# Output of a sparse-attention and mixture-of-experts kernel gathered per token chunk as whole rows, and written after the last column block

## The chip, the cores and the metric

One core of one Trainium2 chip. The metric is the device time of one execution in microseconds, as the median of several runs. The tensor engine (TensorE, PE in the rows), the vector engine (VectorE, DVE), the scalar engine (ScalarE, ACT), GpSimd (POOL) and the sync engine (SyncE, SP), whose queue issues all of this kernel's transfers, run beside each other and wait for one another by semaphores.

## The reference

Attention over 4 batches, 8 heads, 576 positions and 64 dimensions, half of the heads with a local mask, half with a strided one. Its output `x` (2304 tokens, 512 columns) goes through a dense layer pair and then through a soft mixture of experts, whose end is what the change is about:

```python
h = x @ w_in
g = h * (1.0 / (1.0 + np.exp(-1.702 * h)))
x = g @ w_out                                   # 2304 x 512
logits = x @ phi                                # 2304 x 32
d = softmax over the tokens of logits
slot_input = d.T @ x                            # 32 x 512
for e in range(8):                              # 4 slots per expert
    slot_out[e] = np.maximum(slot_input[e] @ w1[e], 0.0) @ w2[e]
c = softmax over the slots of logits
out = c @ slot_out                              # 2304 x 512, float32
```

## The kernel before, in words

Attention and the first dense layer run over five chunks of tokens (`CHUNKS`: four of 512 and one of 256). The slots' sums are gathered on the way, so that the last 55 us hold only the experts and the combination. There the work is set by the order in which the program is written; nothing reorders it but a scheduler that places TensorE's instructions by their readiness.

- The expert weights come in 32 tiles `ex` of 1 MiB (128 partitions, 8 KB each), loaded by SyncE's queue (line 487) as buffers come free. Tiles 4 to 19 of the list are the first expert layer (`expand1`, line 639), tiles 20 to 35 the second (`expand2`, line 669).
- The second layer is cut into three column blocks of the 512 output columns (`COLS`: 256, 128 and 128 wide) that use eight, four and four tiles. In the code `half` counts these blocks, 0 to 2. When a block's tiles are done, `slot_out` (lines 674 and 675) turns the sums into the slot outputs `so`, stored in the tile `fin`, first on ScalarE, then on VectorE.
- `combine` then multiplies the tokens' weights `cT0`/`cT1` (transposed by `combine_t`, cast out of PSUM at line 626) by `so`: one matmul per 128 tokens and column block (line 686), into PSUM tiles `fp` of 512 columns, three buffers of them. Each `fp` is copied to SBUF, in turn by ScalarE (line 689) and VectorE (line 691), and written to `out` (line 692).
- A call of `combine` takes two or four groups of 128 tokens (`PARTS` for the first two blocks, `LAST` for the third) and a staging slot from `gx_tile`, which hands out four regions of the tile `gT` in rotation. Five calls per block, so 15 calls use the four regions in turn, and the copy into a region waits until the region's earlier write has landed.
- A write has rows of 1 KB (block 0) or 512 B (blocks 1 and 2) in `out`, with 128 consecutive tokens on the 128 partitions.
- The combination of block 0 stands between the tiles of block 1, that of block 1 between the tiles of block 2, that of block 2 at the end.

Of the kernel before, what the change touches and what calls it, by code (L numbers as in the profile page):

```python
# [9 lines left out]
F32 = mybir.dt.float32  # L10
# [9 lines left out]
NT, DM, FF = B * S, 512, 2048  # L20
# [9 lines left out]
CHUNKS = [(0, 512), (512, 512), (1024, 512), (1536, 512), (2048, 256)]  # L30
NF = FF // 128
TFROM = 5
COLS = [(0, 256), (256, 128), (384, 128)]
PARTS = [(0, 2), (2, 4), (6, 4), (10, 4), (14, 4)]
LAST = [(0, 4), (4, 4), (8, 4), (12, 4), (16, 2)]
# [6 lines left out]
def tile_kernel(ctx: ExitStack, tc: tile.TileContext, lqk, lv, sqk, sv, wraw, phi, wexp, cst, out):  # L42
    nc = tc.nc
    P = 128
# [4 lines left out]
    xp = ctx.enter_context(tc.tile_pool(name="xp", bufs=3))  # L49
# [302 lines left out]
    side, st, todo = [], {}, []  # L352
# [123 lines left out]
    def gx_tile():  # L476
        k = gxn[0] % 4
        gxn[0] += 1
        return gt[0][:, 4 * k:4 * k + 4]
# [95 lines left out]
    c = len(CHUNKS) - 1  # L575
# [26 lines left out]
    cT0 = tl.tile([P, 2048], F32R, name="cT0")  # L602
# [3 lines left out]
    def ttile(name):  # L606
        return ps_t.tile([P, 512], F32, tag="t", name=name)
# [13 lines left out]
    def combine_t(c):  # L621
        c0, N = CHUNKS[c]
        ctp = ttile(f"ctp_{c}")
        for tt in range(N // 128):
            nc.tensor.transpose(ctp[:, 128 * tt:128 * tt + 128], c4s[c][:, 128 * tt:128 * tt + 128], ident)
        nc.scalar.copy(cT0[:, c0:c0 + N] if c < 4 else cT1, ctp[:, :N])

    hzt = e1p.tile([P, 2, 8, P], F32, tag="e", name="hz")
    hc = e1p.tile([P, 4, 512], F32, tag="e", name="hc")
# [28 lines left out]
    ops, obs = [], {}  # L658

    def expand2(half, n):  # L660
        c0, w = COLS[half]
        per = DM // w
        if n == 0:
            ops.append(mtile(f"op_{half}"))
        t = ex[20 + c0 // 32 + n].rearrange("p j f -> p (j f)").rearrange("p (k j f) -> p k j f", k=per, j=4)
        for k in range(per):
            G, fc = (per * n + k) // 8, (per * n + k) % 8
            for j in range(4):
                nc.tensor.matmul(ops[half][32 * j:32 * j + 32, :w], hz[G][:, fc, 32 * j:32 * j + 32], t[:, k, j], start=G + fc == 0, stop=G + fc == 8)  # L669

    def slot_out(half):
        c0, w = COLS[half]
        o = ops[half][:, :w]
        nc.scalar.mul(so[:, 0, c0:c0 + w], o, zc[:, 0:1])
        nc.vector.scalar_tensor_tensor(so[:, 1, c0:c0 + w], o, zc[:, 1:2], so[:, 0, c0:c0 + w].bitcast(F32), op0=ALU.mult, op1=ALU.add)

    def combine(half, k, n):
        c0, w = COLS[half]
        per = DM // w
        ob = gx_tile().rearrange("p a b -> p (a b)")[:, :n * w].rearrange("p (t f) -> p t f", f=w)  # L680
        for a in range(0, n, per):
            z = min(n, a + per)
            fp = ttile(f"fp_{half}_{k}_{a}")[:, :w * (z - a)].rearrange("p (t f) -> p t f", f=w)
            for t in range(a, z):
                tok = P * (k + t)
                nc.tensor.matmul(fp[:, t - a], cT0[:, tok:tok + P] if k + t < 16 else cT1[:, tok - 2048:tok - 2048 + P], so[:, 1, c0:c0 + w], start=True, stop=True)
            obs[0] = not obs.get(0)
            if obs[0]:
                nc.scalar.copy(ob[:, a:z], fp)
            else:  # L690
                nc.vector.tensor_copy(ob[:, a:z], fp)
        nc.sync.dma_start(out[P * k:P * (k + n), c0:c0 + w].rearrange("(t p) f -> p t f", p=P), ob)

    expand1(0, 0)
    hz = [hzt[:, 0], hzt[:, 1]]
# [11 lines left out]
    for c in range(2):  # L707
        combine_split(c)
        combine_t(c)
# [10 lines left out]
    so, cT1 = fin[:, :2], fin[:, 2, :256]  # L720
    hidden_t(1, 0)
    for n in range(8):
        expand2(0, n)
        if n == 2:
            hidden_t(1, 1)
        if n >= 5:
            combine_split(n - 3)
            combine_t(n - 3)
    slot_out(0)
    for half in range(1, len(COLS)):  # L730
        todo = list(PARTS)
        tiles = COLS[half][1] // 32
        for n in range(tiles):
            expand2(half, n)
            if n:
                for _ in range(-(-len(todo) // (tiles - n))):
                    combine(half - 1, *todo.pop(0))
        slot_out(half)
    for k, n in LAST:
        combine(len(COLS) - 1, k, n)  # L740


def _layouts(q, k, v, w_in, w_out, phi, w1, w2):
# [63 lines left out]
```

## Time and profile before

| | us |
|---|---|
| median of three runs | 442.29 |
| lowest, highest | 441.05, 443.08 |
| profiled execution | 440.19 |
| its span, first to last instruction | 438.4 |
| TensorE busy in the span | 413.0 (94%) |
| VectorE, ScalarE, GpSimd busy | 264.4, 194.1, 77.2 |
| moved by DMA | 80.90 MB |

The span is measured inside the profiled execution, and 1.8 us of that execution lie around it. TensorE's busy time is an average over stages with different limits; what the change is worth is read from the last 30 us alone. Times in the rows are microseconds from the span's start, and durations of single instructions are in ns where a view says so.

### The profile page before, as it was taken

How to read it: one execution, taken by the hardware profiler on the slowest of the kernel's cores; microseconds unless marked ns; L12 is line 12 of the kernel's file. 1: busy time of each engine (PE TensorE's matmuls, PEld its weight loads, DVE VectorE, ACT ScalarE, POOL GpSimd, SP SyncE). 2: the span in 40 equal slices, each digit the busy share in tenths (PEclk: the TensorE clock that was granted, in tenths of full speed). 3: DMA queues.
4: the chain of work that ended last, by engine and by line, in shares of the span. 5: the costliest groups of instructions: out<-in, count | busy, mean ns of one | idle time of the engine just before them, and what ended most of it. 6: DMA issues, size and time to landing. Idle time of an engine off the chain costs nothing.

```text
span 438.4 us, 10081 instructions
## 1 busy us (share of the span) xinstructions
PE 413.0 (94%) x4085; PEld 282.0 (64%) x4085; DVE 264.4 (60%) x564; ACT 194.1 (44%) x640; POOL 77.2 (18%) x96
## 2 busy tenths in 40 slices
PE   8978998998899999999999999999999999899965
PEld 4646575656466767677676776776777796244654
DVE  2789989998996554565467546546454664431212
ACT  2874877766664644454543355331122222120312
POOL 0444445555531110100100001000000000100000
PEclk9999999999999999999999999999999999999995
DMA  8957667676753030321411101770003898979998
GB/s 245 362 169 243 224 201 257 232 239 224 236 171 121 1 101 2 91 78 56 154 42 58 38 1 37 270 305 1 1 0 108 298 381 324 346 310 428 426 351 250
DMA packets 25614, 80.90 MB, mean 185 GB/s; under 512 B 2144, under 2 KB 9440, under 8 KB 21472
## 3 DMA queue, kind: packets, MB, share of 16 engines
q1 hardware_dynamic: 25568, 80.26, 52.2%
q8 instruction: 32, 0.52, 0.5%
q14 instruction: 14, 0.11, 0.1%
HBM read 71.34 MB, written 8.91 MB: 183 GB/s over the span
## 4 chain that ended last, share of the span: by engine, by line
PE 69%; DVE 10%; ACT 8%; DMA 4%; POOL 4%; issue 4%; ACTq 0%; POOLq 0%; DVEq 0%
PE h L321 38%; PE u L435 5%; PE s L163 4%; DMA out<-gT 4%; ACT ts L181 4%; PE lg L340 4%; PE hp L639 3%; DVE wc L264 3%; PE op L669 2%; PE av L218 2%; PE ptp L199 2%; POOL ts L184 2%; PE busy L78 2%; DVE wc L265 2%; POOL wc L262 1%
## 5 line engine op out<-in xcount | busy, mean ns | idle before, releaser
L321 PE MATMUL h<-x,wi 128*128 128x512 f32 (+1 forms) x960 | 224.5, 380 | 4.4 <-POOL wi L273 1.7
L321 PEld LDWEIGHTS h<-x,wi 128*128 128x128 f32 x960 | 161.6, 189 | 54.1 <-issue 13.8
L325 DVE SCALAR_TENSOR_TENSOR gT<-gT,h 128x512 f32<-128x512 f32 (+1 forms) x64 | 40.6, 634 | 61.9 <-ACT gT L324 61.2
L324 ACT ACTIVATE gT<-h 128x512 f32<-128x512 f32 (+1 forms) x64 | 35.6, 556 | 68.1 <-PE h L321 66.4
L181 ACT ACTIVATE ts<-ts,nmx 128x64 f32<-128x64 f32 (+1 forms) x120 | 41.6, 349 | 28.6 <-DVE nmx L176 28.2
L184 POOL TENSOR_TENSOR ts<-ts,sm 128x384 f32<-128x384 f32 (+2 forms) x32 | 27.9, 873 | 139.2 <-DVE sm L183 65.4
L348 DVE STREAM_TRANSPOSE gT<-gT 128x512 f32<-128x512 f32 (+1 forms) x64 | 41.0, 649 | 0.9
L262 POOL TENSOR_SCALAR wc<-wc 128x512 f32<-128x512 f32 x32 | 24.5, 765 | 28.4 <-ACT wc L261 26.0
L340 PE MATMUL lg<-gT,wp 128*32 128x512 f32 (+1 forms) x128 | 26.9, 564 | 0.3 <-ACT wp L297 0.3
L264 DVE SCALAR_TENSOR_TENSOR wc<-raw,wc 128x512 uint32<-128x512 uint32 x32 | 26.0, 817 | 0.4
L265 DVE SCALAR_TENSOR_TENSOR wc<-raw,wc 128x512 uint32<-128x512 uint32 x32 | 25.4, 794 | 0.3
L163 PEld LDWEIGHTS s<-qk 64*64 64x64 f32 x552 | 20.9, 133 | 6.4 <-issue 5.0
L163 PE MATMUL s<-qk 64*64 64x96 f32 (+1 forms) x552 | 25.0, 235 | 0.0
L273 POOL TENSOR_TENSOR wi<-wc,wi 128x512 fp32r<-128x512 f32 x16 | 22.2, 1388 | 15.5 <-ACT wi L272 15.3
L243 ACT CAST x<-av 128x320 fp32r<-128x320 f32 (+20 forms) x54 | 19.1, 395 | 13.0 <-DVE x L244 9.6
L261 ACT ACTIVATE wc<-raw 128x512 f32<-128x512 f32 x32 | 21.7, 678 | 5.7 <-DMA raw<-wraw 5.6
L263 DVE TENSOR_SCALAR wc<-wc 128x512 uint32<-128x512 uint32 x32 | 20.1, 628 | 6.6 <-POOL wc L262 6.5
L182 DVE TENSOR_SCALAR sm<-sm 128x5 f32<-128x5 f32 (+2 forms) x32 | 6.8, 213 | 27.5 <-ACT ts L181 27.5
L181 ACT ACTIVATION_READ_ACCUMULATOR ts<-ts,nmx 128x1 f32 x120 | 22.6, 188 | 0.0
L199 PE MATMUL ptp<-cs,ts 128*96 128x128 f32 (+1 forms) x120 | 17.7, 280 | 4.9 <-POOL ts L184 4.5
L435 PE MATMUL u<-gT,dT 32*32 32x512 f32 x576 | 20.2, 597 | 2.1 <-DVE z L410 2.1
L697 POOL MEMSET hz<- 128x512 f32 x4 | 2.1, 560 | 110.7 <-PE spp L592 110.7
(124 smaller groups left out, 472.6 us busy)
## 6 DMA issues: line engine op xcount, KB each, us to landing
ex<-wexp SPq DMA_DIRECT2D x28, 1024.0 KB, 7.9
raw<-wraw SPq DMA_DIRECT2D x32, 512.0 KB, 4.4
qk<-lqk SPq DMA_DIRECT2D x8, 592.0 KB, 5.4
wo_scr<-wc SPq DMA_DIRECT2D x16, 256.0 KB, 2.9
ex<-wo_scr SPq DMA_DIRECT2D x4, 1024.0 KB, 9.2
gT<-wexp SPq DMA_DIRECT2D x4, 1024.0 KB, 5.8
qk<-sqk SPq DMA_DIRECT2D x6, 604.0 KB, 4.1
v<-lv SPq DMA_DIRECT2D x8, 432.0 KB, 4.5
```

Of the source, the lines that this page charges most:

```text
L163: nc.tensor.matmul(sp[hs, u], t[hs, qo:qo + 64], t[hs, ko + qo:ko + qo + nk], start=not early, stop=not early or u == nt - 1)
L181: nc.scalar.activation(ts[:, u], src[:, u], AF.Exp, scale=sc, bias=nmx[:, u:u + 1], accum_out=sm[:, u:u + 1])
L184: nc.gpsimd.tensor_tensor(ts, ts, sm[:, :nt].unsqueeze(2).to_broadcast([P, nt, nk]), op=ALU.mult)
L262: nc.gpsimd.tensor_scalar(t, t, F64_LARGE, F64_SMALL, op0=ALU.min, op1=ALU.max)
L264: nc.vector.scalar_tensor_tensor(u, raw[:, :, 1], 0xC0000000, u, op0=ALU.bitwise_and, op1=ALU.bitwise_or)
L265: nc.vector.scalar_tensor_tensor(u, raw[:, :, 0], 29, u, op0=ALU.logical_shift_right, op1=ALU.bitwise_or)
L321: nc.tensor.matmul(h[:, :N], w[:, we, 128 * kt:128 * kt + 128], x[xe][:, kt, :N], start=n == 0, stop=n == 11)
L324: nc.scalar.activation(g[:, :N], h[:, :N], AF.Tanh, scale=0.851)
L325: nc.vector.scalar_tensor_tensor(g[:, :N], g[:, :N], 1.0, h[:, :N], op0=ALU.add, op1=ALU.mult)
L340: nc.tensor.matmul(lgs[c][32 * j:32 * j + 32, :N], wp[:, f0 + j, :], gs[c, f0 + j][:, :N], start=f0 == 0, stop=f0 == NF - 4)
L348: nc.vector.transpose(t_slots(c)[:, f, :N], gs[c, f][:, :N])
L435: nc.tensor.matmul(us[a][32 * j:32 * j + 32, :].rearrange("p (t f) -> p t f", f=32), dT[q, 32 * b:32 * b + 32], gT[q, :, 32 * b:32 * b + 3 ...
```

## The change

`combine` now takes a chunk of tokens instead of a list of groups. Each of the five chunks has a region of its own for its output, which holds all 512 columns: the four regions of `gT` for the chunks of 512 tokens, and a new tile `ob_last` for the chunk of 256. All three column blocks are copied into it, and the write is issued when the third has been copied. The tokens of a chunk are dealt to the partitions differently: partition p holds the four tokens 4p to 4p+3 of the chunk (two in the last), so that a partition's part of `out` is one stretch of 8 KB (4 KB). For that, `combine_t` stores the columns of `cT0` and `cT1` in another order, while they are cast.

```diff
-        nc.scalar.copy(cT0[:, c0:c0 + N] if c < 4 else cT1, ctp[:, :N])
+        t = cT0[:, c0:c0 + N] if c < 4 else cT1
+        nc.scalar.copy(t.rearrange("k (t p) -> k p t", p=P), ctp[:, :N].rearrange("k (p t) -> k p t", p=P))
...
-    def combine(half, k, n):
+    def combine(half, c):
         c0, w = COLS[half]
-        per = DM // w
-        ob = gx_tile().rearrange("p a b -> p (a b)")[:, :n * w].rearrange("p (t f) -> p t f", f=w)
-        for a in range(0, n, per):
-            z = min(n, a + per)
-            fp = ttile(f"fp_{half}_{k}_{a}")[:, :w * (z - a)].rearrange("p (t f) -> p t f", f=w)
+        t0, N = CHUNKS[c]
+        ntt, per = N // 128, DM // w
+        if half == 0:
+            obs[c] = gx_tile() if c < 4 else xp.tile([P, 2, 512], F32, tag="x0", name="ob_last")
+        ob = obs[c]
+        for a in range(0, ntt, per):
+            z = min(ntt, a + per)
+            fp = ttile(f"fp_{half}_{c}_{a}")[:, :w * (z - a)].rearrange("p (t f) -> p t f", f=w)
             for t in range(a, z):
-                tok = P * (k + t)
-                nc.tensor.matmul(fp[:, t - a], cT0[:, tok:tok + P] if k + t < 16 else cT1[:, tok - 2048:tok - 2048 + P], so[:, 1, c0:c0 + w], start=True, stop=True)
-            obs[0] = not obs.get(0)
-            if obs[0]:
-                nc.scalar.copy(ob[:, a:z], fp)
+                nc.tensor.matmul(fp[:, t - a], cT0[:, t0 + P * t:t0 + P * t + P] if c < 4 else cT1[:, P * t:P * t + P], so[:, 1, c0:c0 + w], start=True, stop=True)
+            obs["n"] = not obs.get("n")
+            if obs["n"]:
+                nc.scalar.copy(ob[:, a:z, c0:c0 + w], fp)
             else:
-                nc.vector.tensor_copy(ob[:, a:z], fp)
-        nc.sync.dma_start(out[P * k:P * (k + n), c0:c0 + w].rearrange("(t p) f -> p t f", p=P), ob)
+                nc.vector.tensor_copy(ob[:, a:z, c0:c0 + w], fp)
+        if half == len(COLS) - 1:
+            nc.sync.dma_start(out[t0:t0 + N].rearrange("(p t) f -> p t f", t=ntt), ob[:, :ntt])
...
     for half in range(1, len(COLS)):
-        todo = list(PARTS)
+        todo = list(range(len(CHUNKS)))
...
-                    combine(half - 1, *todo.pop(0))
+                    combine(half - 1, todo.pop(0))
         slot_out(half)
-    for k, n in LAST:
-        combine(len(COLS) - 1, k, n)
+    for c in range(len(CHUNKS)):
+        combine(len(COLS) - 1, c)
```

The change moves instructions on two engines that matter for the end. On SyncE's queue, this is the end of the program, as a piece of the difference (before with -, changed with +; the sizes are partitions by elements, and a first dimension after the partitions counts the token groups):

```order
-L692 DMA out<-gT 128x2x256
-L692 DMA out<-gT 128x4x256 x4
-L692 DMA out<-gT 128x2x128
-L692 DMA out<-gT 128x4x128 x8
-L692 DMA out<-gT 128x2x128
-L803 UNCONDITIONAL_BRANCH
+L696 DMA out<-gT 128x2048 x4
+L696 DMA out<-ob_last 128x1024
+L807 UNCONDITIONAL_BRANCH
```

Fifteen writes have become five, and the loads of the weight tiles ahead of them are the same. The five are issued after copies of the last column block, where before one third of the calls (five) was.

On TensorE, this is the stretch from the last tile of column block 1 (`op_4478`) over the four tiles of block 2 (`op_4586`; `ex_4335` to `ex_4368`) to the first groups after them, before the change (the names `fp_0_0` and so on count the first token group and the group within the call):

```order
L669 MATMUL op_4478<-ex_4333,hz 32x128 x16
L686 MATMUL fp_0_0_4619<-fin,cT_4215 128x128 x2
L686 MATMUL fp_2_0_4624<-fin,cT_4215 128x128 x4
L669 MATMUL op_4586<-ex_4335,hz 32x128 x16
L669 MATMUL op_4586<-ex_4337,hz 32x128 x16
L669 MATMUL op_4586<-ex_4366,hz 32x128 x16
L669 MATMUL op_4586<-ex_4368,hz 32x128 x16
L686 MATMUL fp_6_0_4647<-fin,cT_4215 128x128 x4
L686 MATMUL fp_10_0_4654<-fin,cT_4215 128x128 x4
L686 MATMUL fp_14_0_4677<-fin,cT_4215 128x128 x2
L686 MATMUL fp_14_0_4677<-fin 128x128 x2
L686 MATMUL fp_0_0_4686<-fin,cT_4215 128x128 x4
```

And the same stretch now (here the names count the chunk, and `op_4582` is block 2):

```order
L670 MATMUL op_4478<-ex_4333,hz 32x128 x16
L689 MATMUL fp_0_0_4615<-fin,cT_4215 128x128 x4
L689 MATMUL fp_1_0_4621<-fin,cT_4215 128x128 x2
L670 MATMUL op_4582<-ex_4335,hz 32x128 x16
L689 MATMUL fp_1_0_4621<-fin,cT_4215 128x128 x2
L689 MATMUL fp_2_0_4643<-fin,cT_4215 128x128 x4
L689 MATMUL fp_3_0_4649<-fin,cT_4215 128x128 x3
L670 MATMUL op_4582<-ex_4337,hz 32x128 x16
L689 MATMUL fp_3_0_4649<-fin,cT_4215 128x128
L689 MATMUL fp_4_0_4671<-fin 128x128 x2
L670 MATMUL op_4582<-ex_4366,hz 32x128 x16
L670 MATMUL op_4582<-ex_4368,hz 32x128 x16
```

All 18 matmuls of block 1's combination now stand ahead of the last two tiles; before, 12 of them stood behind the last.

## Rows read from the trace of the kernel before

**Rows 1.** The page's span in 40 slices: TensorE's busy tenths and GB/s moved.

```profile
PE   8978998998899999999999999999999999899965
...
GB/s 245 362 169 243 224 201 257 232 239 224 236 171 121 1 101 2 91 78 56 154 42 58 38 1 37 270 305 1 1 0 108 298 381 324 346 310 428 426 351 250
```

**Rows 2.** The chain that ended last, its end: start us, us, what.

```profile
415.51 12.18 DMA out<-gT
...
427.77 0.59 ACT gT L689
...
428.38 3.15 DMA out<-gT
...
432.25 2.61 DMA out<-gT
```

**Rows 3.** Waits from 410 us to the end: total us, times, longest.

```profile
DVE gT L691 <- DMA out<-gT: 12.2, 6, 6.7
...
ACT gT L689 <- DMA out<-gT: 6.8, 5, 2.1
```

**Rows 4.** Windows: length, each engine's busy us, then TensorE's clock, DMA share, GB/s.

```profile
395.00:419.00 24.00, 22.82 (x346) 13.07 (x339) 5.27 (x18) 5.12 (x10) 0.00 (x0) 1.00 1.02 425
419.00:421.50 2.50, 2.50 (x87) 2.43 (x90) 0.00 (x0) 0.00 (x0) 0.00 (x0) 1.00 0.98 268
422.50:424.50 2.00, 0.20 (x8) 0.21 (x12) 0.00 (x0) 0.00 (x0) 0.00 (x0) 1.00 1.08 386
428.50:432.50 4.00, 3.51 (x15) 3.13 (x15) 1.47 (x3) 1.17 (x2) 0.00 (x0) 0.50 0.65 199
432.50:437.00 4.50, 1.88 (x9) 1.69 (x8) 1.30 (x2) 0.96 (x2) 0.00 (x0) 0.50 1.14 344
```

**Rows 5.** Timeline of TensorE: start us, us, instructions, idle before and its releaser.

```profile
412.20 0.97 PE L686 MATMUL fp<-fin,cT 128*128 128x256 f32 x6
...
416.00 0.50 PE L686 MATMUL fp<-fin 128*128 128x256 f32 x2
...
418.39 0.89 PE L686 MATMUL fp<-fin,cT 128*128 128x128 f32 x6 [0.87 <-DVE fin L675]
419.21 2.83 PE L669 MATMUL op<-ex,hz 128*32 128x128 f32 x96
424.30 1.08 PE L669 MATMUL op<-ex,hz 128*32 128x128 f32 x32 [2.26 <-DMA ex<-wexp]
```

**Rows 6.** Timeline of ScalarE and VectorE, the same columns.

```profile
410.46 0.36 ACT L626 CAST fin<-ctp 128x256 fp32r<-128x256 f32 x1
...
412.74 1.07 ACT L689 COPY gT<-fp 128x512 f32<-128x512 f32 x2 [1.92 <-PE fp L686]
...
425.85 0.35 DVE L675 SCALAR_TENSOR_TENSOR fin<-op,cs,fin 128x128 fp32r<-128x128 f32 x1
```

**Rows 7.** SyncE's issues (start us), each single one followed by KB and us to landing.

```profile
387.00 0.33 SPq L487 DMA_DIRECT2D ex<-wexp  x1
...
ex<-wexp SPq DMA_DIRECT2D x1, 1024.0 KB, 4.8
...
399.61 0.33 SPq L487 DMA_DIRECT2D ex<-wexp  x1
...
ex<-wexp SPq DMA_DIRECT2D x1, 1024.0 KB, 20.6
...
402.33 0.33 SPq L487 DMA_DIRECT2D ex<-wexp  x1
...
ex<-wexp SPq DMA_DIRECT2D x1, 1024.0 KB, 21.9
...
413.36 22.47 SPq L692 DMA_DIRECT2D out<-gT  x15
...
435.35 0.47 SPq L692 DMA_DIRECT2D out<-gT  x1
...
out<-gT SPq DMA_DIRECT2D x1, 128.0 KB, 2.1
```

## The prediction

> **What bounds the kernel now.** I read the 40 slices of the page first. From slice 31 on (340 us) the row of GB/s stays near 300 to 430 and ends in 351 and 250, while TensorE falls to 6 and 5 tenths: the end belongs to DMA [rows 1]. The chain that ended last says the same: from 415.51 us it consists of three waits for `out` transfers (12.18, 3.15 and 2.61 us) with one copy of 0.59 us between them [rows 2]. Then I read who waits: in the last 30 us VectorE stood 12.2 us and ScalarE 6.8 us in front of copies whose staging slot was still being written out [rows 3]. Taken alone, this row promises up to several microseconds to a kernel that gives each chunk a slot of its own.
>
> The windows tell how the transfers themselves went, and they are what I build on [rows 4]. From 395 to 419 us the weight tiles `ex` arrive at 425 GB/s with the engines busy all the time (share 1.02). From 419 to 421.5 us, with the first 1 KB rows of `out` queued behind them since 413.36 us [rows 7], the engines are as busy (0.98), yet only 268 GB/s move. From 422.5 to 424.5 us, nearly all 1 KB rows, it is 386 GB/s. From 428.5 to 432.5 us the engines have work only 0.65 of the time (199 GB/s): there the slots are waited for. From 432.5 to 437 us, all 512 B rows, it is 344 GB/s. So three things cost DMA time before: mixed traffic, short rows, and 4 us of half idle queue.
>
> **The change, part by part.**
>
> *Casts at old line 626.* Five, with the same number of elements, now written with a step of 512 B. No row shows such a cast of these shapes. The last one ends at 410.8 us, and the first matmuls that need its chunk run at 416.0 us [rows 6, 5], so even a doubled cast is covered: 0. If that cover were gone, it would cost at most its own length again.
>
> *Copies into row slots.* Nine, five and five copies as before, of the same size, alternating between the two engines. A copy takes 0.59 us on ScalarE [rows 2]. They no longer wait for a write, because no write is issued between them. Their sources are three PSUM buffers, as before.
>
> *Matmuls that move forward.* Before, TensorE does 6 of the 18 matmuls of column block 1 (0.89 us from 418.39), then three weight tiles (2.83 us), and waits until 424.30 for the last tile; the other 12 come after it, because their copies wait for slots [rows 5, 3]. Now all 18 stand ahead of the last two tiles. Weight loads set the pace: (419.21 - 418.39) / 6 = 0.137 us each, so 12 x 0.137 = 1.6 us more ahead of the last tile: TensorE is ready for it at 419.21 + 2.83 + 1.6 = 423.6 us instead of 422.0.
>
> *The last tile's arrival.* The last two tiles landed at 399.61 + 20.6 = 420.2 and 402.33 + 21.9 = 424.2 us [rows 7], 4.0 us apart, where 1 MiB at 425 GB/s takes 2.47 us. The excess of 1.5 us falls into the 268 GB/s stretch [rows 4]. Without writes behind the loads I take the cadence: 420.2 + 2.5 = 422.7 us. Bounds: 422.7 and, if the slow stretch has another cause, the old 424.2. In the first case TensorE decides (423.6), in the second the tile (424.3). I take 423.6; the gain is 0.7 us, the bounds are 0 and 0.7.
>
> *From the last tile to the first write.* The tile costs 1.08 us; before, it ended at 425.38 and VectorE had the slot output at 425.85 + 0.35 = 426.20 [rows 5, 6], so 0.82 us later. Four matmuls, then a copy: between the first matmul at 412.20 and the copy at 412.74 lie 0.54 us, for two wide ones; for four narrow ones I take 0.65, and the copy 0.59 us [rows 5, 6, 2]. 423.6 + 1.1 + 0.8 + 0.65 + 0.6 = **426.7 us** for the first issue (upper bound 427.4). The other four chunks follow faster than the 2.5 us that DMA needs for one, even where the granted clock is 0.50 (1.2 GHz), as it is from 428.5 us on [rows 4]; they cost nothing.
>
> *The writes.* Before, 15 of them, the first issued at 413.36, the last at 435.35 and landed 2.1 us later at 437.45; the span ended 0.95 us after that [rows 7]. Now five, none before 426.7 us, and all 4.72 MB are behind that point. What was hidden under column blocks 1 and 2 is so no longer: this is the price. What comes back are the 199 GB/s stretch and the short rows. The trace has no write with 8 KB per row. Nearest in row size are the loads, 8 KB per partition, 425 GB/s [rows 4]; nearest in direction are the 1 KB rows at 386. Since rows of 512 B, 1 KB and 8 KB stand at 344, 386 and 425, I take 425: 4.72 / 0.425 = 11.1 us. Fixed part: the last 128 KB took 2.1 us, of which 0.131 / 0.344 = 0.4 are data, which leaves 1.7: 12.8 us in all. A load stream from a standing start gives more: its first 1 MiB took 4.8 us [rows 7], and 3.5 more at 2.47 make 13.4. I take the middle, **13.1 us**; bounds 12.8 and, at 344 GB/s with 1.7, 15.4.
>
> On this rate the Trainium skill speaks against the change: its page "DMA: Bandwidth & Descriptors", section "Where 436 GB/s comes from", holds that transfers between HBM and SBUF are bound by HBM at about 358 GB/s per core. The rows contradict it for loads (425 for 24 us); no row here shows it for long rows of writes. An estimate by that page's figure is 4.72 / 0.358 = 13.2 us of data in place of 11.1, about 2.1 us more than my sum.
>
> **Sum.** 426.7 + 13.1 + 0.95 = 440.75 us of span against 438.4: **+2.35 us**. The profiled execution took 440.19 us, so 442.5 on its scale; it lies 0.5% under the median of the three runs, 442.29, and on the scale of the median I say 442.29 + 2.35 = **444.6 us**. A measurement of this kernel can tell about 0.5% (2.2 us) from no change: the forecast stands just beyond that.
>
> **The rivals.**
>
> *Not slower: the moved matmuls are hidden.* If the 12 matmuls cost under 0.7 us together, TensorE is waiting when the last tile lands at 422.7, the first write goes at 425.8, and the end is 425.8 + 13.1 + 0.95 = 439.85: +1.5 us, 443.8; with the short fixed part +1.2 us, 443.5. It decides from 0.06 us per moved matmul downwards, or where the fill of the write stream is short. For it: rows of matmuls overlap their weight loads. Against it: 0.137 us per matmul in the only row of this shape at full clock [rows 5]. Smaller fixed costs lead to the same place, so I give this side 0.34.
>
> *Slower by more: writes do not run at the loads' rate.* At 386 GB/s the data take 12.2 us (+1.1, 445.8), at 344 GB/s 13.7 us (+2.6, 447.2). For it: no write row above 386. Against it: the rate rises with the row size in every row shown, and the 8 KB rows of the loads sustain 425. The Trainium skill's page named above would put it here too. 0.17.
>
> *Faster: the waits for slots were the bound.* The 199 GB/s stretch wastes 4 x (344 - 199) / 344 = 1.7 us; gone without a price it would give 440.6, and with faster rows a little less. But the price is there: to end 2.2 us earlier, at 436.2, the whole output would have to go from first issue to landing in 436.2 - 0.95 - 426.7 = 8.55 us, so 4.72 MB in under 7 us, near 690 GB/s; the fastest slices of the page are under 430 [rows 1]. It decides only if the first write goes before about 422.3 us, where TensorE is still at column block 2. 0.07.
>
> That the writes might still go early is excluded by the order of SyncE's queue: all five stand behind the last load, and each needs a copy of the last column block.
>
> **How the numbers follow.** Forecast (+2.2 to +3.3, the last tile on time or late): 0.42; rival one 0.34; rival two 0.17; rival three 0.07. Faster by over 0.5%: 0.07; within: 0.34; slower: 0.42 + 0.17 = 0.59. The range goes from 442.8 (the lower side of rival one, with a quarter of it left out) to 447.2 (344 GB/s).
>
> **What would show it.** Right: no wait of a copy for `out`; the load stream at about 425 GB/s up to its end near 422.7 us without a 268 GB/s dip; TensorE starting the last tile at about 423.6 without a wait for `ex`; the first write issued near 426.7; a gap in the GB/s between 423 and 427.5; then some 11 us above 400 GB/s, and a chain that ends in one DMA wait of about 13 us behind one copy. Wrong: a write stream under 390 GB/s, a last tile that still lands at 424, or a first issue before 425.

## The result, and the profile after

The changed kernel took 444.69 us (median of 18 runs, 442.64 to 446.08) against 442.19 us before (18 runs): a ratio of 1.0056, with a 95% interval of 1.0039 to 1.0073. It is slower, by 2.5 us; 444.6 was forecast. Run once more beside the experiments it gave 1.0075 (1.0058 to 1.0092). The profiled execution took 442.64 us, with a span of 440.9.

On the page, the GB/s of the last slices now show a hole (146 in the last slice but one) where before there was none [rows 1], and TensorE is done a slice earlier:

```profile
span 440.9 us, 10051 instructions
...
PE   8978998999899999999999999999999998999970
...
GB/s 245 360 178 245 208 216 239 255 243 194 254 158 112 1 98 8 85 92 42 153 63 37 38 20 19 332 240 1 0 0 182 307 381 366 291 323 424 424 146 358
```

The windows of the last stretch, with the columns of [rows 4], which they answer to:

```profile
395.00:419.00 24.00, 22.92 (x344) 12.95 (x336) 6.06 (x19) 5.73 (x10) 0.00 (x0) 1.00 1.01 425
419.00:421.50 2.50, 2.50 (x47) 2.23 (x45) 0.75 (x2) 0.50 (x1) 0.00 (x0) 1.00 0.68 288
422.50:424.50 2.00, 2.00 (x64) 1.75 (x56) 0.42 (x1) 0.58 (x1) 0.00 (x0) 1.00 0.03 8
424.50:428.00 3.50, 2.63 (x41) 2.33 (x33) 1.04 (x2) 1.37 (x3) 0.00 (x0) 1.00 0.00 0
428.00:438.40 10.40, 0.32 (x2) 0.18 (x2) 0.69 (x1) 0.54 (x2) 0.00 (x0) 0.64 1.00 421
```

The loads run at the same 425 GB/s. From 419 to 421.5 us the rate is low again, but for another reason than before: the DMA share is 0.68, not 0.98, so the loads are running out, not slowed. Then the queue is empty for 5.5 us (8 and 0 GB/s), and then the whole output goes at 421 GB/s. Before, some 2.34 MB were left at 428.5 us (199 GB/s for 4 us and 344 for 4.5 us, [rows 4]) and took 8.6 us; now 4.72 MB are left at 428.0 us and take 11.2 us at 421 GB/s. The difference of these ends, 439.2 against 437.1 us, is 2.1 of the 2.5 us by which the spans differ; the other 0.4 us lie behind the last byte.

TensorE's timeline answers to [rows 5]; its first row here, the last two matmuls of column block 0, serves below as a mark:

```profile
416.31 0.50 PE L689 MATMUL fp<-fin 128*128 128x256 f32 x2
...
418.69 0.89 PE L689 MATMUL fp<-fin,cT 128*128 128x128 f32 x6 [0.87 <-DVE fin L676]
419.51 1.08 PE L670 MATMUL op<-ex,hz 128*32 128x128 f32 x32
420.52 1.22 PE L689 MATMUL fp<-fin,cT 128*128 128x128 f32 x9
...
423.16 1.96 PE L670 MATMUL op<-ex,hz 128*32 128x128 f32 x64
425.99 2.00 PE L689 MATMUL fp<-fin,cT 128*128 128x128 f32 x16 [0.87 <-DVE fin L676]
```

It no longer waits for a weight tile: the last two tiles run back to back from 423.16 us. SyncE's rows answer to [rows 7]; the last load landed at 402.42 + 20.2 = 422.6 us, before at 424.2:

```profile
402.42 0.33 SPq L487 DMA_DIRECT2D ex<-wexp  x1
...
ex<-wexp SPq DMA_DIRECT2D x1, 1024.0 KB, 20.2
...
427.30 3.36 SPq L696 DMA_DIRECT2D out<-gT  x4
430.75 1.20 SPq L696 DMA_DIRECT2D out<-ob_last  x1
...
out<-ob_last SPq DMA_DIRECT2D x1, 512.0 KB, 9.0
```

The waits from 410 us on that answer to [rows 3]: both engines' copies wait for TensorE only, and no wait for `out` is left in the view.

```profile
ACT gT L692 <- PE fp L689: 8.9, 6, 2.7
...
DVE gT L694 <- PE fp L689: 7.0, 8, 1.9
```

### The profile page after: what moved, and what is told of

Same layout as the page of the kernel before. It is cut to its first block, busy times and chain, and to the rows that moved or that the text cites. A ratio compares the mean times of both kernels' runs of the same rounds, so it can differ in the third digit from the quotient of the medians.

```text
span 440.9 us, 10051 instructions
## 1 busy us (share of the span) xinstructions
PE 409.4 (93%) x4085; PEld 279.1 (63%) x4085; DVE 264.6 (60%) x564; ACT 195.8 (44%) x640; POOL 77.4 (18%) x96
## 4 chain that ended last, share of the span: by engine, by line
PE 67%; DVE 10%; ACT 8%; issue 6%; POOL 4%; DMA 2%; SPq 0%; POOLq 0%; ACTq 0%; DVEq 0%
PE h L321 38%; PE u L435 5%; ACT ts L181 4%; PE s L163 4%; PE lg L340 4%; PE op L670 4%; PE hp L640 3%; DVE wc L264 3%; PE av L218 2%; PE ptp L199 2%; POOL ts L184 2%; DMA qk<-lqk 2%; PE fp L689 2%; POOL wc L262 2%; DVE wc L265 2%
## 5 line engine op out<-in xcount | busy, mean ns | idle before, releaser
L435 PE MATMUL u<-gT,dT 32*32 32x512 f32 x576 | 20.2, 597 | 2.1 <-DVE z L410 2.1
```

The costliest lines, as they stand in the source:

```text
L435: nc.tensor.matmul(us[a][32 * j:32 * j + 32, :].rearrange("p (t f) -> p t f", f=32), dT[q, 32 * b:32 * b + 32], gT[q, :, 32 * b:32 * b + 3 ...
```

## The experiments

Two measures are given for each. The ratio to the kernel before, with its 95% interval, decides. Beside it stands the **last stretch** of the profiled execution, from the start of the last two matmuls of column block 0 to the end of the span. It is 438.4 - 416.00 = 22.4 us before and 440.9 - 416.31 = 24.6 us after.

What lies ahead of the mark is nearly the same work in all versions, and the mark stands between 416.0 and 419.0 us. Two things move it. The combination of column block 0, from its first matmul to the mark, takes 3.80 us in both profiles of the kernel before (416.00 - 412.20 in the first) and 4.20 us in every version of the changed kernel (416.31 - 412.11), so the last stretch leaves out 0.4 us that the change costs. And every profile whose mark stands at 417.9 us or later has a stretch ahead of it with a granted clock below 1.00, while the other four, with marks from 416.0 to 416.7 us, have none. In the second profile of the changed kernel the clock is 0.50 (1.2 GHz) from 375.5 to 378.5 us, with TensorE busy throughout; in its first profile it is 1.00 (2.4 GHz) there. The spans of the four undisturbed profiles can be compared as they are, and they agree with the ratios: 438.4 us before, 440.9 changed, 441.4 with rows of 2 KB, 436.9 in two parts with the tokens dealt as before.

| version | ratio, 95% interval | mark to end | last stretch, us |
|---|---|---|---|
| changed kernel | 1.0056 (1.0039 to 1.0073) | 416.31 to 440.9 | 24.6 |
| changed kernel again | 1.0075 (1.0058 to 1.0092) | 417.96 to 442.5 | 24.5 |
| own regions, 15 writes when copied | 1.0002 (0.9987 to 1.0016) | 418.29 to 439.9 | 21.6 |
| two parts, tokens as changed | 0.9978 (0.9962 to 0.9995) | 418.86 to 439.4 | 20.5 |
| 15 writes, meant to be held back | 1.0002 (0.9982 to 1.0023) | 418.43 to 440.0 | 21.6 |
| matmuls moved back | 1.005 (1.0028 to 1.0072) | 418.44 to 442.1 | 23.7 |
| rows of 2 KB | 1.0086 (1.0067 to 1.0104) | 416.19 to 441.4 | 25.2 |
| block 0 early, tokens as before | 0.9992 (0.9971 to 1.0013) | 418.00 to 438.7 | 20.7 |
| two parts, tokens as before | 0.9959 (0.9932 to 0.9987) | 416.68 to 436.9 | 20.2 |

The theory (H) was that the price of the change is the hold-back of the writes; the rivals were that the slots (S) or the row length (R) decide.

### Own regions, each column block written when it is copied

```diff
-        if half == len(COLS) - 1:
-            nc.sync.dma_start(out[t0:t0 + N].rearrange("(p t) f -> p t f", t=ntt), ob[:, :ntt])
+        nc.sync.dma_start(out[t0:t0 + N, c0:c0 + w].rearrange("(p t) f -> p t f", t=ntt), ob[:, :ntt, c0:c0 + w])
```

> The change with one part undone: the regions of their own stay, but each column block of a chunk is written as soon as it is copied (15 writes, rows of 1 KB and 512 B as before). Theory H (what costs is holding the writes back: the DMA queue stands idle from the last tile at 422.6 us to the first write packet at 428.0): the queue has work from the end of the loads on. 2.36 MB at 386 GB/s and twice 1.18 MB at 344 are 13.0 us from 421.4, so the span ends near 435.8, ratio to before about 0.994; the dip in the loads' rate around 420 us comes back. Rival S (own regions and fewer waits are all that changed the time, and when a write is issued does not matter): as the changed kernel, 1.0056. Rival R (short rows are what costs, the hold-back is free): slower than the changed kernel by 1.9 us, 1.010.

The ratio is 1.0002: the loss of the change is gone, with the regions and the dealing of tokens kept, and with short rows. S and R both fall. H keeps its direction, not its number: 0.994 was expected. Its windows, with the columns of [rows 4], show where it fell short:

```profile
419.00:421.00 2.00, 1.13 (x35) 0.86 (x23) 0.53 (x2) 0.79 (x2) 0.00 (x0) 1.00 1.05 430
421.00:423.00 2.00, 2.00 (x42) 1.73 (x41) 0.69 (x1) 0.02 (x1) 0.00 (x0) 1.00 1.03 290
...
425.00:430.00 5.00, 4.13 (x83) 3.75 (x83) 1.47 (x3) 1.97 (x4) 0.00 (x0) 1.00 1.09 377
431.00:437.00 6.00, 0.00 (x0) 0.00 (x0) 0.00 (x0) 0.00 (x0) 0.00 (x0) 0.50 1.05 315
```

The dip is back, as expected: 290 GB/s at a DMA share of 1.03, when writes stand behind the last loads. From 431 to 437 us, with rows of 512 B, the mean is 315 GB/s, not 344. That is no rate of these rows: it is 293 GB/s up to 433.5 us, at a DMA share of 0.97, and 345 at a share of 1.15 from there to 436.5 us, as before the change. The dip did not delay TensorE here: the last tile starts 7.84 us after the mark (425.15 + 0.98 - 418.29), in the changed kernel 7.83.

### Two parts

Blocks 0 and 1 of a chunk together when block 1 is copied, block 2 at the end:

```diff
-        if half == len(COLS) - 1:
-            nc.sync.dma_start(out[t0:t0 + N].rearrange("(p t) f -> p t f", t=ntt), ob[:, :ntt])
+        if half:
+            f0 = 0 if half == 1 else c0
+            nc.sync.dma_start(out[t0:t0 + N, f0:c0 + w].rearrange("(p t) f -> p t f", t=ntt), ob[:, :ntt, f0:c0 + w])
```

> As the changed kernel, but column blocks 0 and 1 of a chunk are written together (rows of 1.5 KB) when block 1 is copied, and block 2 (rows of 512 B) at the end. Theory H: 3.54 MB go out from about 421 us at some 395 GB/s (between 386 for 1 KB and 425 for 8 KB), 9.0 us, until 430.0, then 1.18 MB at 344 GB/s, 3.4 us, so landing near 433.8 and a span near 434.8; ratio 0.992, the fastest of all versions. Rival R (row length decides): between the changed kernel and before, 1.002 to 1.008. If the queued writes slow the last tile as before, up to 1 us of the gain is lost: 0.994.

0.9978, below the whole range that rival R allowed, and faster than the kernel before: H again, and again short of its number. Its rows of 512 B, with the tokens dealt the new way, run as fast as those of the kernel before (344 GB/s, [rows 4]):

```profile
433.00:435.00 2.00, 0.00 (x0) 0.00 (x0) 0.00 (x0) 0.00 (x0) 0.00 (x0) 0.56 1.14 349
```

### Fifteen writes, meant to be held back

```diff
         if half == len(COLS) - 1:
-            nc.sync.dma_start(out[t0:t0 + N].rearrange("(p t) f -> p t f", t=ntt), ob[:, :ntt])
+            for f0, n in COLS:
+                nc.sync.dma_start(out[t0:t0 + N, f0:f0 + n].rearrange("(p t) f -> p t f", t=ntt), ob[:, :ntt, f0:f0 + n])
```

> As the changed kernel, with all writes held back to the same point, but each chunk in three writes of 256, 128 and 128 columns (rows of 1 KB and 512 B). It measures the row length alone, with nothing else moved. Theory H: 13.0 us of data in place of 11.1, so 1.9 us more than the changed kernel: span near 442.8, ratio 1.010. If the rate of the writes is set by something other than the rows, it stays at 1.0056; if issuing 15 transfers limits it, over 1.012.

This run did not test what it was made for. Its writes stand at the end of the program's text, but the scheduler places a write by the copies it reads, and two of three read only column block 0 or 1. SyncE's row shows the first at 415.76 us:

```profile
415.76 18.55 SPq L697 DMA_DIRECT2D out<-gT  x12
434.35 2.04 SPq L697 DMA_DIRECT2D out<-ob_last  x3
```

So it is one more version with early writes and short rows, and it gives what the first of them gave: 1.0002 and 21.6 us. Short rows with all writes held back stay untried.

### The moved matmuls put back

```diff
-        todo = list(range(len(CHUNKS)))
+        todo = list(range(len(CHUNKS) if half == 1 else 2))
...
     for c in range(len(CHUNKS)):
+        if c > 1:
+            combine(1, c)
         combine(len(COLS) - 1, c)
```

> The changed kernel with the matmuls of column block 1 of chunks 2, 3 and 4 (10 of the 18) moved back behind the last tile of block 2. Writes as in the changed kernel. If the moved matmuls delay the last tile (as the prediction's sum has it), TensorE waits for the last tile, which lands at 422.6, starts it there instead of at 424.1, and the first write is issued at 425.8 instead of 427.3; the five writes then end 1.4 us earlier: span 439.5, ratio 1.0025. If the moved matmuls were hidden, the time stays at 1.0056, or grows because copies for chunks 2 to 4 are then late.

TensorE's timeline in this version:

```profile
418.44 0.50 PE L689 MATMUL fp<-fin 128*128 128x256 f32 x2
...
425.15 1.08 PE L670 MATMUL op<-ex,hz 128*32 128x128 f32 x32 [0.18 <-DMA ex<-wexp]
427.11 3.00 PE L689 MATMUL fp<-fin,cT 128*128 128x128 f32 x24 [0.87 <-DVE fin L676]
```

TensorE now reaches the last tile before it has landed and waits 0.18 us. The last tile starts 6.71 us after the mark, in the changed kernel 424.14 - 416.31 = 7.83 (half of the 64 matmuls from 423.16). The first write is issued at 428.56 us, 10.1 us after the mark in place of 427.30 - 416.31 = 11.0, so 0.9 us sooner, and the last stretch is 0.9 us shorter. That is the sum's term, at two thirds of the expected 1.4 us, read from one profile of each. The ratios, 1.005 against 1.0056 and 1.0075, point the same way, but their intervals overlap.

### The changed kernel again, and with rows of 2 KB

> The changed kernel once more, beside the three below, so that all stand on the same runs. Every theory: 1.0056 within 0.002; the last 25 us (from the last group of column block 0 to the end) 24.6 us long, as in its first profile.

24.5 us and 1.0075: within 0.002 of the first measurement.

```diff
-        nc.scalar.copy(t.rearrange("k (t p) -> k p t", p=P), ctp[:, :N].rearrange("k (p t) -> k p t", p=P))
+        nc.scalar.copy(t, ctp[:, :N])
...
-            nc.sync.dma_start(out[t0:t0 + N].rearrange("(p t) f -> p t f", t=ntt), ob[:, :ntt])
+            nc.sync.dma_start(out[t0:t0 + N].rearrange("(t p) f -> p t f", p=P), ob[:, :ntt])
```

> The changed kernel with the tokens on the partitions as before (128 consecutive tokens on the partitions) and the plain cast: five writes at the same point, rows of 2 KB in place of 8 KB (4 KB). It measures what the new dealing of tokens to partitions is worth. If the rate depends on the row length, the rate lies between 386 GB/s (1 KB) and 425 (8 KB), say 405, the data take 11.6 us in place of 11.1, and the time is 0.5 us above the changed kernel: 1.0067. If 2 KB is long enough, 1.0056, as the changed kernel. The shorter casts (0.59 in place of 1.09 us) give nothing either way.

The writes went at 407 GB/s in place of 421, as the window shows:

```profile
428.50:439.50 11.00, 0.00 (x0) 0.00 (x0) 0.10 (x1) 0.11 (x1) 0.00 (x0) 0.61 1.05 407
```

4.72 MB at 407 are 11.6 us, 0.4 more than at 421; the last stretch is 0.7 us longer, the ratio 0.001 higher than that of the changed kernel beside it. The rate moved as expected; the time moved by less than the intervals can tell. By the medians and the last stretches, the new dealing of tokens together with its strided cast is worth some half a microsecond; that is not clear of the noise.

### Block 0 early, and two parts, with the tokens dealt as before

Both stand on the version with rows of 2 KB. Block 0 early:

```diff
-        if half == len(COLS) - 1:
-            nc.sync.dma_start(out[t0:t0 + N].rearrange("(t p) f -> p t f", p=P), ob[:, :ntt])
+        if half != 1:
+            f0, f1 = (0, w) if half == 0 else (COLS[1][0], DM)
+            nc.sync.dma_start(out[t0:t0 + N, f0:f1].rearrange("(t p) f -> p t f", p=P), ob[:, :ntt, f0:f1])
```

> Own regions, tokens as before, column block 0 written when copied (rows of 1 KB), blocks 1 and 2 together at the end (rows of 1 KB). Theory H (the idle queue between the loads and the first write is what the change costs): block 0's 2.36 MB at 386 GB/s take 6.1 us and fill just that gap; the other 2.36 MB follow from 428.1 on, 6.1 us more, a span near 435.6 on the scale of the profile of before (438.4): ratio 0.994. The versions with early writes that ran so far came out 1 to 2 us later than so computed; then 0.997. Theory R (row length decides): as the changed kernel or above it, 1.0056 to 1.010.

0.9992, so clear of the changed kernel and of rival R, and not told from the kernel before. Its windows:

```profile
421.00:422.50 1.50, 1.50 (x38) 1.23 (x37) 0.69 (x1) 0.00 (x0) 0.00 (x0) 1.00 0.93 251
423.00:428.50 5.50, 4.63 (x110) 4.02 (x110) 1.47 (x3) 1.34 (x4) 0.00 (x0) 1.00 1.07 377
428.50:430.00 1.50, 1.50 (x13) 1.34 (x12) 0.97 (x2) 1.05 (x2) 0.00 (x0) 1.00 0.67 232
430.00:436.00 6.00, 0.01 (x1) 0.00 (x0) 0.41 (x1) 0.37 (x1) 0.00 (x0) 0.70 1.09 385
```

Block 0 fills the hole, at the price of the dip (251 GB/s), and leaves a short hole before the last part (232 GB/s).

Two parts, with the tokens as before:

```diff
+        if half:
+            f0 = 0 if half == 1 else c0
+            nc.sync.dma_start(out[t0:t0 + N, f0:c0 + w].rearrange("(t p) f -> p t f", p=P), ob[:, :ntt, f0:c0 + w])
```

> Two parts as before-last (blocks 0 and 1 together in rows of 1.5 KB when block 1 is copied, block 2 in rows of 512 B at the end), but with the tokens on the partitions as in the kernel before. In the first run of two parts the issue of one write took 0.6 to 1.8 us on SyncE's queue and the last 1.18 MB went at about 320 GB/s, where the kernel before shows 0.37 us and 344 GB/s. If that came from the dealing of the tokens, this version gains about 1 us on it: 0.9955. If not, it stays at 0.9978.

0.9959 (0.9932 to 0.9987), median 439.82 us: the fastest version, clear of both kernels. Its windows:

```profile
419.00:421.00 2.00, 1.94 (x39) 1.68 (x40) 0.70 (x2) 0.00 (x0) 0.00 (x0) 1.00 0.95 397
421.00:424.00 3.00, 3.00 (x62) 2.66 (x66) 1.06 (x2) 1.17 (x2) 0.00 (x0) 1.00 0.92 351
424.00:430.00 6.00, 3.81 (x74) 3.37 (x64) 1.79 (x4) 1.91 (x4) 0.00 (x0) 1.00 1.06 394
430.00:432.50 2.50, 0.00 (x0) 0.00 (x0) 0.00 (x0) 0.00 (x0) 0.00 (x0) 0.59 1.12 357
```

The first part is copied just as the loads end, so there is no 290 GB/s stretch with a full queue, and hardly a hole: 397, 351, 394 and 357 GB/s from 419 to 432.5 us, with half a microsecond (421.0 to 421.5 us) at 103. Whether the plain dealing gained on the other version with two parts stays open: the intervals overlap. It did not do so by the rate of the last part, as the expectation had it: rows of 512 B ran at 347 GB/s here (431 to 433.5 us) and at 349 there.

### The kernel before, once more

> The kernel before once more, for a second profile of its last stretch. From the last matmuls of column block 0 to the end it took 22.4 us in the first profile; the versions with early writes took 0.8 to 2.2 us less by that measure, but their medians gained 0.4 to 1 us less than that. If the first profile's stretch was a long one by chance, this one is 21.5 to 22 us; if it is 22.4 again, the difference lies ahead of the stretch.

The second profile has its mark at 418.97 us and its end at 441.9, a stretch of 22.9 us. TensorE waits twice for a tile there:

```profile
418.97 0.50 PE L686 MATMUL fp<-fin 128*128 128x256 f32 x2
...
424.80 1.08 PE L669 MATMUL op<-ex,hz 128*32 128x128 f32 x32 [0.68 <-DMA ex<-wexp]
427.83 1.08 PE L669 MATMUL op<-ex,hz 128*32 128x128 f32 x32 [1.96 <-DMA ex<-wexp]
```

So the first profile's stretch was not a long one by chance. The early versions gain 0.4 to 1.3 us less in the medians than in their last stretches. Of this, 0.4 us are the longer combination of block 0 ahead of the mark; the rest is open. It does not come with early writes, since the changed kernel and the two other versions with late writes lose 0.3 to 1.2 us more in the medians than in their last stretches.

## Why the prediction was right

**What bounds the end: right.** The end stayed with DMA, and the waits for slots, 12.2 and 6.8 us in the view of waits, were worth little by themselves: the version with its own regions and early writes has none of them left either, and takes as long as the kernel before (1.0002). That it is the hold-back and not the regions, the token dealing or the row length is shown by the versions that keep the regions and write early: the five versions that write a part early lie between 0.9959 and 1.0002, the three that write nothing before the last column block between 1.005 and 1.0086, and no interval of the one group reaches into the other.

**The load stream: right.** The dip at a full queue left with the early writes and came back with them (290 and 251 GB/s); the last tile landed at 422.6 us, 422.7 was forecast. The rate did not hold up to that landing, as the prediction's sign had it: it stayed between 393 and 426 GB/s until 420.5 us and then fell to 98, with a DMA share of 0.24, while the last bytes came in.

**From the last tile to the first write: 0.6 us too early.** 426.7 was forecast, 427.30 came. The mark itself came 0.3 us later: a term that the sum left out, since the combination of block 0 in its new order takes 4.20 us up to the mark in place of 3.80, and it started 0.1 us sooner. The moved matmuls cost 5.45 - 3.65 = 1.8 us (from the first matmul of block 1 to the start of the last tile, 418.69 to 424.14 against 418.39 to 422.04) in place of 1.6. The rest, 0.1 us, lies in the steps behind the tile.

**The writes: 0.65 us too long.** 13.1 us were forecast, 430.75 + 9.0 - 427.30 = 12.45 came; the lower bound was 12.8. The rate was the step that I had to choose between 344 and 425, and 421 came. The longer fixed part taken from the loads' first megabyte was not there: 4.72 / 0.421 = 11.2 leaves 1.25 us, less than the 1.7 of the last write before. This mis-sized term and the one above it cancel: that the total came within 0.2 us is luck in the sizes, not in the mechanism. The end of the span behind the last landing took 1.1 us in place of 0.95.

**The rule on HBM.** The Trainium skill, "DMA: Bandwidth & Descriptors", "Where 436 GB/s comes from", would have had the writes at about 358 GB/s. The rows show 421 for 10.4 us, so the trace disagrees here as it did for loads. The section gets its figure by halving the rate of a stack that two cores share; this program runs on one core, and no run here shows what a second one would take away.

**The rivals.** The moved matmuls were not hidden: 10 of the 18 put back give 0.9 us in the profile, and that version is still slower than before. The slower write rate and the gain from the waits did not come. The view of the chain did not show the long DMA wait that I had named as its end; it stops at the last copy, at 428.73 us, and the writes behind it are read from the windows and from SyncE's rows. The lower end of the range, 442.8 us, follows from no sum of the prediction: rival one's own times are 443.5 and 443.8 us.

## What to carry to other kernels

Ask of a merged transfer first when its last part is ready, and what the queue does until then: here 5.5 us of empty queue cost more than rows of 8 KB and the end of all slot waits gave back. A wait for a staging slot on an engine that is not the bottleneck says little; count the bytes that are left when the last piece of work starts, and divide by the rate of their rows. Split the merge so that its first part is ready just when the loads end (here two parts, 0.9959 and 0.9978) and not later, where the queue runs dry. Earlier, writes queue behind loads and slow them; the three versions that wrote earlier have the higher medians (0.9992 to 1.0002), but their intervals overlap with those of the two parts.

## What the runs showed of the hardware that was not expected

- Writes queued behind loads on the same queue slow the loads: with the DMA share near 1, the rate falls from 425 to 268 (before), 290 and 251 GB/s, and it doesn't where no write is queued. With the first write issued between 413 and 417 us the last tile landed 3.0 to 4.0 us after the one before it (five profiles); where the first write came at 420.5 us or later, 2.3 to 2.5 us (six profiles).
- The rate of writes by row length, from the windows: 512 B 344 (349 with the tokens dealt the new way), 1 KB 385, 1.5 KB 394, 2 KB 407, 8 KB 421 GB/s.
- The cast that writes with a step of 512 B took 1.8 times as long as the plain one: the view of tile `ctp` in the changed kernel shows 1062 to 1092 ns for 128x512, where the same view of the kernel before has 586 to 588.

```profile
L627 ACT CAST cT<-ctp x4: 1062/1075/1092, 383.3 to 409.0; 128x512 fp32r<-128x512 f32 x4
```
